# Eight shared PSUM banks, global scores on 544 columns, and another order for the last batch of a fused attention and mixture kernel

## Chip, cores and metric

The kernel runs on one core of a Trainium2 chip. The metric is device time in microseconds (us) for one execution; lower is better. Engines are named as in the profile: PE (matmul; PEld is its weight load), DVE, ACT, POOL, and SP, which issues DMAs. The profile comes from one execution; the times come from others.

## What is computed

Two stages for 8 batches, all in f32. The first is attention with 8 heads of 64 dimensions: 512 local positions see 32 global positions and a band of 32 to each side; 32 global positions see everything. The second takes the 544 x 512 result through four experts of causal attention with 64 dimensions each, of which the two with the highest gate values count.

```python
# stage 1, per batch and head (scale = 1/8)
s_g  = scale * q_g @ concat(k_g, k_l).T            # 32 x 544, no mask
out_g = softmax(s_g) @ concat(v_g, v_l)
s_l  = concat(scale * q_l @ k_g.T, where(|i-j| <= 32, scale * q_l @ k_l.T, -1e9))
out_l = softmax(s_l) @ concat(v_g, v_l)
x = concat(out_g, out_l)                           # 544 x 512 over the heads
# stage 2, per batch
gates = top-2 softmax of x @ w_gate
for e in range(4):
    a = softmax(causal(scale * (x @ wq[e]) @ (x @ wk[e]).T))
    out += gate[e] * (a @ (x @ wv[e]) @ wo[e])
```

## The kernel before

**Order.** The kernel first records every operation with `op` (engines allowed, planned ns, a function, the buffers it reads and writes, a priority), and then `Plan.place` issues them one by one. PE's operations are issued in exactly the order in which they were written. For DVE, ACT, POOL and SP the planner picks, by its planned times, the operation that could start first, ties going to the lower priority. Each engine then runs its queue in that order on the chip, waiting by semaphores. Planned times set the order alone.

**Buffers.** A `Ring` has so many slots, and a `Buf` takes a slot when its first operation is placed and gives it back after its last. PSUM has eight banks of 512 f32 per partition. Before the change they are two rings: `sc`, two buffers of two banks each, for the scores of stage 1 (`sp`) and 2 (`msp`); and `w`, four buffers of one bank for all else:

```python
    sc_ring, w_ring = Ring(2, loose=True), Ring(4, loose=True)
    def scores(name):
        return Buf(sc_ring, lambda: psum.tile([128, 2, 512], F32, tag="sc", name=name, bufs=2))
    def ps(shape, name):
        return Buf(w_ring, lambda: psum.tile(shape, F32, tag="w", name=name, bufs=4))
```

**Steps.** `step(s)` writes stage 1 for pair s of heads (32 pairs, four to a batch) and, six steps later, stage 2 of a batch in four steps r = 0 to 3, with the rest of the batch before (`old`) still to be done: scores of its second two experts (c = 1) in r = 0 and 1, products in r = 1 and 3, outputs in r = 3. Within a step, `whole` weaves short transposes (`turns`) among long projections (`products`).

**Stage 1 of a pair.** `kn` and `qn` become `kd` and `qp` (DVE's 32x32 transposes; in the first four pairs PE's `px`). `kd` holds groups of 96 local keys and the 32 global keys again (POOL copies `kg` there), 128 columns a group, so that 96-wide windows and the global keys are one operand. PE: `sp` (L515). DVE takes the band and the row minimum of each 128 columns (L527), ACT the exponential (L530). A step later PE transposes (`pt`, L545), ACT or DVE copies to `ptw` (L238 for ACT, L240 for DVE; all copies have these lines), and a step after that PE forms `xq` (L564), DVE scales it to `xn` (L568), PE turns it (`xp`, L579), and ACT and DVE split it into high and low parts `xh` (L249) and `xl` (L250). The values `v` are spread by POOL copies (L240).

**Global queries.** Every second step, `p1_global_scores` multiplies two pairs' global queries (`qb`) with the 640 columns of `kd` (`spg`, L625): 512 columns in one bank, in which the global keys come again in groups 1 to 3 and are masked out by `gmask` (DVE, L628), and 128 in another (L632). ACT's exponential covers 640 columns (L637). `long_turn` transposes five chunks of 128 (`pga`, L653), copied to `longt`; `p1_global_av` (L674) multiplies with `v`.

**Stage 2 of a batch.** `pqk` (L704) gives `kt`, `qt`; `pv` (L741, L752) the values; `m_gates` a chain of small DVE operations on `xt` (L777 to L806), with the ranking at L784 to L791. The score tiles t = 0, 1, 2 of a pair of experts hold the query blocks (0 and 1), (2), (3), so 128 and 256, 384 or 512 columns: PE `msp` (L833), DVE `pm` with the causal mask (L847), ACT's exponential (L851), DVE's sums and reciprocals `msm` (L854, L856), POOL's scaling with the gate (L862), PE's `mpt` (L886), copies to `mptw`, PE's `yp` (L905), ACT's `yh` and DVE's `yl`. The last 32 positions of all four experts, the tail, take their own way: `tsp` (L926, DVE L929 and L933), one exponential (L941), `long_turn`, `yt` (L965), `turned` (L591), `tt` (L597), `yth`, `ytl`. `out_tile` multiplies with `wo` (`po`, L984), ACT copies (`ot`) and issues the output DMA (L991): four tiles a batch, and a tail tile for four batches with four DMAs.

**The end.** After the last batch's r = 3 there is nothing left to lie beside it. It writes in this order: tail product, all of `yp` for c = 1, the tail's turn, four output tiles, the tail's output tile.

Of the kernel before, what the change touches and what calls it, by code (L numbers as in the profile page):

```python
# [1 line left out]

# [192 lines left out]
def fused_kernel(ctx: ExitStack, tc: tile.TileContext, q_l, k_l, v_l, q_g, k_g, v_g,  # L195
# [144 lines left out]

    def setup_gmask():
        def f(e):
            nc.gpsimd.memset(gmask, 0.0)
            nc.gpsimd.memset(gmask[:, 1:, 96:], NEG)
        op("POOL", 800, f, w=["gmask"])
# [155 lines left out]
    def p1_scores(k):  # L501
# [6 lines left out]
        def f(e):  # L508
            for t in range(4):
                for g in range(4):  # L510
                    u = 4 * t + g
                    c = col(window(u))
                    for h in range(2):
                        rows = slice(64 * h, 64 * h + 64)
                        nc.tensor.matmul(sp.t[32 * g:32 * g + 32, h, 128 * t:128 * t + 128],  # L515
                                         qp.t[rows, 32 * u:32 * u + 32], kd.t[rows, c:c + 128],
                                         start=True, stop=True)
# [91 lines left out]
    def p1_global_scores(b, g):  # L609


        qb = G[b]["qb"]
        sg = buf("long", [128, 5, 128])
        sm = buf("sgm", [128, 8], 3)
        kdl = [PR[b * NP + 2 * g + j]["kd"] for j in range(2)]
        for half in range(2):
            sp = ps([128, 4 - 3 * half, 128], "spg")

            def f(e, half=half, sp=sp):
                for j in range(2):  # L620
                    p, kd, out_ = 2 * g + j, kdl[j].t, sp.t[64 * j:64 * j + 64].rearrange("p c s -> p (c s)")
                    parts = [(out_, kd[:, :512])] if half == 0 else [(out_[:, :96], kd[:, 512:608]),
                                                                     (out_[:, 96:], kd[:, 640:])]
                    for o_, k_ in parts:
                        nc.tensor.matmul(o_, qb.t[:, p, :], k_, start=True, stop=True)  # L625
            op("PE", 950 - 700 * half, f, r=[qb, *kdl], w=[sp])
            if half == 0:
                op("DVE", 610, lambda e, sp=sp: nc.vector.tensor_tensor_reduce(  # L628
                    out=sg.t[:, :4], in0=sp.t, in1=gmask, scale=-SCALE, scalar=BIG,
                    op0=ALU.add, op1=ALU.min, accum_out=sm.t[:, 0:1]), r=[sp, "gmask"], w=[(sg, 0), (sm, 0)])  # L630
            else:
                op("DVE", 210, lambda e, sp=sp: nc.vector.tensor_scalar(  # L632
                    sg.t[:, 4], sp.t[:, 0], -SCALE, None, op0=ALU.mult, op1=ALU.min, accum_out=sm.t[:, 1:2]), r=[sp],
                   w=[(sg, 1), (sm, 1)])
        op("DVE", 100, lambda e: nc.vector.tensor_reduce(sm.t[:, 2:3], sm.t[:, 0:2], axis=AX.X, op=ALU.min),
           r=[(sm, 0), (sm, 1)], w=[(sm, 2)], late=20)
        op("ACT", 825, lambda e: nc.scalar.activation(sg.t, sg.t, AF.Exp, bias=sm.t[:, 2:3], scale=-1.0,  # L637
                                                      accum_out=sm.t[:, 3:4]), r=[sg, (sm, 2)], w=[sg, (sm, 3)], late=30)
# [517 lines left out]
```

## Time and profile before

| | |
|---|---|
| median of 3 runs (lowest, highest) | 554.78 us (554.69, 556.05) |
| profiled execution: own time, span | 553.77 us, 552.0 us |
| mean clock granted to PE | 0.994 of full |
| DMA: packets, MB | 190792, 41.83 |
| PE's idle time, summed over the windows 0:50, 50:500, 500:530, 530:552 | 14.6, 16.1, 0.6, 8.0 us |

Instructions carry the line of `kernel.py` and the program's names, `out<-in`. A timeline row is: start, length, engine, line, operation, names, shape, count, and in brackets how long the engine had been idle and what ended that. A waits row is: who waited, for whom, us in total, times, longest. PE's ends are modelled, so matmuls overlap in the rows. In the trace an f32 matmul is two instructions of PE (a transpose is one).

### The profile page before, as it was taken

The numbers are of one execution on the slowest core, as the hardware profiler recorded it, in microseconds if no ns is written. First come the engines' busy times: TensorE is split into PE (matmuls) and PEld (weight loads), VectorE is DVE, ScalarE is ACT, GpSimd is POOL, SyncE is SP. The second block draws the span as 40 slices with busy tenths as digits, with TensorE's granted clock in tenths as the row PEclk, the third lists the DMA queues.
The fourth block names the chain that finished last, engine by engine and source line by source line (L and its number), as shares of the span: only waits on it lengthen the run. The fifth ranks groups of instructions, "written<-read, shape, count | busy, mean of one in ns | idle before, by whom it ended". The sixth has DMA issues, their size and how long they took to land.

```text
span 552.0 us, 22219 instructions
## 1 busy us (share of the span) xinstructions
PE 512.7 (93%) x8796; PEld 425.4 (77%) x8796; DVE 413.8 (75%) x1713; ACT 323.2 (59%) x1146; POOL 287.7 (52%) x526
## 2 busy tenths in 40 slices
PE   4887999899999999998999999999999999999976
PEld 3666976778878887887878787788878888788754
DVE  6999879778777887779786896778877775565550
ACT  1767548866466745755675763667457464542552
POOL 6988579874193745648175642927437212231230
PEclk9989999999999999999999999999999999999989
DMA  9786585462262513533163422624122000200202
GB/s 178 144 148 129 111 160 101 86 114 42 53 149 55 95 22 70 146 70 50 25 136 87 84 34 57 145 54 78 22 48 80 2 2 2 78 2 1 77 2 95
DMA packets 190792, 41.83 MB, mean 76 GB/s; under 512 B 186080, under 2 KB 186080, under 8 KB 190688
## 3 DMA queue, kind: packets, MB, share of 16 engines
q1 hardware_dynamic: 174448, 29.12, 28.8%
q10 hardware_dynamic: 16240, 11.29, 6.7%
q8 instruction: 69, 1.13, 0.9%
q14 instruction: 35, 0.29, 0.2%
HBM read 31.47 MB, written 8.91 MB: 73 GB/s over the span
## 4 chain that ended last, share of the span: by engine, by line
PE 65%; DVE 11%; ACT 9%; DMA 5%; POOL 4%; issue 3%; SPq 2%; POOLq 0%; DVEq 0%; ACTq 0%
PE pqk L704 13%; PE pv L741 8%; PE po L984 7%; PE msp L833 6%; PE xq L564 5%; PE mpt L886 5%; PE yp L905 4%; PE sp L515 4%; POOL v L240 3%; PE pt L545 3%; PE spg L625 2%; ACT st L530 2%; DMA v<-in_v_l_dram 2%; PE xp L579 2%; PE pga L653 2%
## 5 line engine op out<-in xcount | busy, mean ns | idle before, releaser
L240 POOL COPY v<-v 32x512 f32<-32x512 f32 (+2 forms) x192 | 116.3, 606 | 46.6 <-DMA v<-in_v_l_dram 36.1
L862 POOL TENSOR_SCALAR pm<-pm,msm,gate 128x512 f32<-128x512 f32 (+3 forms) x128 | 76.9, 614 | 119.8 <-DVE msm L856 86.3
L530 ACT ACTIVATE st<-st,sm 128x128 f32<-128x128 f32 x256 | 100.4, 395 | 35.2 <-DVE sm L527 26.9
L240 POOL COPY v<-vg 32x640 f32<-32x640 f32 (+1 forms) x96 | 65.9, 686 | 38.5 <-PE xg L674 26.8
L851 ACT ACTIVATE pm<-pm,msm 128x512 f32<-128x512 f32 (+3 forms) x128 | 70.6, 554 | 22.9 <-DVE msm L847 22.8
L847 DVE CUSTOM_DVE_ANT_0 pm<-msp,cmask 128x512 f32<-128x512 f32 (+3 forms) x128 | 56.9, 486 | 11.2 <-PE msp L833 11.2
L527 DVE CUSTOM_DVE_ANT_0 st<-sp,band 128x128 f32<-128x128 f32 x256 | 58.1, 285 | 9.4 <-PE sp L515 9.4
L886 PE MATMUL mpt<-ident,pm 128*128 128x128 f32 x320 | 48.1, 276 | 7.1 <-DVE kt L240 3.4
L886 PEld LDWEIGHTS mpt<-ident,pm 128*128 128x128 f32 x320 | 36.5, 141 | 16.2 <-POOL pm L862 5.5
L530 ACT ACTIVATION_READ_ACCUMULATOR st<-st,sm 128x1 f32 x256 | 48.7, 190 | 0.0
L833 PE MATMUL msp<-kt,qt 64*64 64x384 f32 (+3 forms) x512 | 46.1, 448 | 0.5 <-DVE qt L240 0.5
L515 PE MATMUL sp<-kd,qp 64*32 64x128 f32 x2048 | 39.6, 283 | 3.9 <-issue 1.8
L564 PEld LDWEIGHTS xq<-v,ptw 128*32 128x32 f32 x2048 | 30.7, 111 | 14.8 <-issue 6.2
L564 PE MATMUL xq<-v,ptw 128*32 128x64 f32 x2048 | 36.2, 223 | 5.6 <-ACT ptw L238 2.7
L905 PE MATMUL yp<-mptw,vt 128*64 128x128 f32 x640 | 40.1, 278 | 0.3 <-issue 0.3
L704 PE MATMUL pqk<-xh,wk_hi 128*128 128x272 f32 x128 | 39.6, 309 | 0.3 <-DVE xl L604 0.3
L545 PE MATMUL pt<-ident,st 128*128 128x128 f32 x256 | 36.4, 274 | 3.5 <-DVE xl L250 3.2
L704 PE MATMUL pqk<-xh,wq_hi 128*128 128x272 f32 x128 | 39.7, 310 | 0.0
L238 ACT COPY mptw<-mpt 128x512 f32<-128x512 f32 (+1 forms) x51 | 23.9, 487 | 26.2 <-PE mpt L886 25.6
L741 PE MATMUL pv<-wv_hi,xh 128*128 128x260 f32 x128 | 38.6, 301 | 0.7 <-DVE xl L250 0.7
L905 PEld LDWEIGHTS yp<-mptw,vt 128*64 128x64 f32 x640 | 36.2, 139 | 1.7 <-issue 0.7
L704 PE MATMUL pqk<-xl,wq_hi 128*128 128x272 f32 x128 | 36.9, 288 | 0.0
(166 smaller groups left out, 1365.9 us busy)
## 6 DMA issues: line engine op xcount, KB each, us to landing
out_dram<-ot ACTq DMA_DIRECT2D x32, 256.0 KB, 2.1
v<-in_v_l_dram SPq DMA_DIRECT2D x62, 120.0 KB, 3.2
kn<-in_k_l_dram SPq DMA_DIRECT2D x109, 64.0 KB, 2.7
qn<-in_q_l_dram SPq DMA_DIRECT2D x109, 64.0 KB, 2.4
v<-in_v_l_dram SPq DMA_DIRECT2D x59, 32.0 KB, 2.5
vg<-in_v_g_dram SPq DMA_DIRECT2D x21, 64.0 KB, 2.2
qn<-in_q_l_dram ACTq DMA_DIRECT2D x5, 128.0 KB, 2.7
ot<-in_q_g_dram SPq DMA_DIRECT2D x8, 64.0 KB, 2.2
```

The costliest lines, as they stand in the source:

```text
L240: ENG[e].tensor_copy(out, in_)
L515: nc.tensor.matmul(sp.t[32 * g:32 * g + 32, h, 128 * t:128 * t + 128], qp.t[rows, 32 * u:32 * u + 32], kd.t[rows, c:c + 128], start=True, ...
L527: op("DVE", 211, lambda e, h=h, t=t, i=i: nc.vector.tensor_tensor_reduce(out=st.t[:, h, t], in0=sp.t[:, h, 128 * t:128 * t + 128], in1=ban ...
L530: op("ACT", 385, lambda e, h=h, t=t, i=i: nc.scalar.activation(st.t[:, h, t], st.t[:, h, t], AF.Exp, bias=sm.t[:, 0, i:i + 1], scale=-1.0, ...
L564: nc.tensor.matmul(xq.t[32 * g:32 * g + 32, t, h, :], pts[h].t[:, 32 * u:32 * u + 32], v.t[:, h, window(u), :], start=True, stop=True)
L704: nc.tensor.matmul(pp.t, w[:, ch, cols], x(part, ch)[:, n], start=(ch == 0 and w is hi and part == 0), stop=(ch == NCH - 1 and part == 1))
L741: nc.tensor.matmul(pv.t, x(part, ch)[:, 128 * i:128 * i + 128], w[:, ch, :], start=(ch == 0 and part == 0 and w is hi), stop=(ch == NCH - ...
L833: nc.tensor.matmul(sp.t[64 * u:64 * u + 64, x, at:at + n], qt.t[rows, q0:q0 + 64], kt.t[rows, :n], start=True, stop=True)
L851: op("ACT", 280 + 0.83 * n, lambda e, x=x, at=at, n=n, s=s: nc.scalar.activation(pm.t[:, x, at:at + n], pm.t[:, x, at:at + n], AF.Exp, bia ...
L862: op("POOL", 240 + 0.83 * n, lambda e, x=x, at=at, n=n, i=i, s=s: nc.gpsimd.tensor_scalar(pm.t[:, x, at:at + n], pm.t[:, x, at:at + n], sm ...
L886: nc.tensor.transpose(pt.t[:, k, :], pm.t[:, x, at + 128 * j:at + 128 * j + 128], ident)
L905: nc.tensor.matmul(yp.t[64 * x:64 * x + 64, 128 * i:128 * i + 128], vt.t[:, j, 64 * (2 * c + x):64 * (2 * c + x) + 64], flat[:, where[x, i ...
```

## The change

There are three parts.

1. One ring of eight banks, made once as fixed tiles. `ps` gives any bank a view of the wanted shape, and `scores` is a list of two such buffers, one for each head (or expert) of the pair. The ring picks the free slot whose planned end is longest ago.
2. The global scores are taken on 544 columns: 416 in the first bank (128 of group 0, then 96 of each of groups 1 to 3, read from `kd` with gaps), 128 in the second. There is no `gmask`; DVE's first operation becomes a `tensor_scalar` with a minimum, as the second was. The exponential covers 544 columns. The transposes are of 128, 96, 96, 96 and 128 columns (`CHUNKS`), and the copy to `longt` is split, since the 96-row chunks fill only 96 partitions; the products over these chunks run over 96 partitions.
3. For the last batch alone: the 384-wide tile of c = 1 is written in r = 0 and not in r = 1; the scaling of its c = 1 probabilities may go to DVE or POOL; `yp` for c = 1 is in two halves with the tail's turn between them; the tail's output tile comes first.

```diff
-                    b.tile = ring.fixed[b.slot] if ring.fixed else b.make()
+                    if ring.fixed:
+                        b.tile = ring.fixed[b.slot]
+                        if b.make:
+                            b.tile = b.make(b.tile)
+                    else:
+                        b.tile = b.make()
...
-    sc_ring, w_ring = Ring(2, loose=True), Ring(4, loose=True)
+    banks = [psum.tile([128, 512], F32, name=f"bank{i}", bufs=1) for i in range(8)]
+    ring = Ring(8, loose=True, fixed=banks)
+    def ps(shape, name):
+        def view(bank):
+            t = bank[:, :math.prod(shape[1:])]
...
+        return Buf(ring, view)
     def scores(name):
-        return Buf(sc_ring, lambda: psum.tile([128, 2, 512], F32, tag="sc", name=name, bufs=2))
+        return [ps([128, 512], name) for _ in range(2)]
...
-        for half in range(2):
-            sp = ps([128, 4 - 3 * half, 128], "spg")
+        for half, n in ((0, 416), (1, 128)):
+            sp = ps([128, n], "spg")
...
+                    if half == 0:
+                        parts = [(o_[:, :128], kd[:, :128]),
+                                 (o_[:, 128:].rearrange("p (c s) -> p c s", s=96),
+                                  kd[:, 128:512].rearrange("p (c s) -> p c s", s=128)[:, :, :96])]
+                    else:
+                        parts = [(o_[:, :96], kd[:, 512:608]), (o_[:, 96:], kd[:, 640:])]
...
+    CHUNKS = ((0, 128), (128, 96), (224, 96), (320, 96), (416, 128))
...
+        rows = min(rows for _, rows in some)
+        evac(lambda: pt.t[:rows, 4 * part:4 * part + n, :], lambda: pa.t[:rows], 128 * n, [pa], [(pt, part)])
+        if rows < 128:
+            evac(lambda: pt.t[rows:, 0, :], lambda: pa.t[rows:, 0, :], 128, [pa], [(pt, "g")])
...
+                engs = "POOL|DVE" if b == B - 1 and c == 1 else "POOL"
...
+        for some in ((0, 1), (2, 3)) if between else (range(4),):
...
+            if between and n0 == 0:
+                between()
...
+        end = r == 3 and old == B - 1
...
-            m_av(old, 1)
+            m_av(old, 1, M[old, "turn"] if end else None)
...
-        if has(first[0]):
+        if has(first[0]) and not (r == 1 and old == B - 1):
...
-                products += [lambda: m_out_tail(old // 4)]
+                products.insert(0 if end else 4, lambda: m_out_tail(old // 4))
...
+        if r == 0 and old == B - 1:
+            m_scores(old, 1, 1)
+            m_softmax(old, 1, 1)
```

**What moves in the queues.** PE's order changes only in the last batch. Its last stretch up to the first output tile was:

```order
L833 MATMUL msp<-kt,qt 64x256 x4
L905 MATMUL yp<-mptw,vt 64x128 x20
L926 MATMUL tsp<-kt,qtbd_78 64x512 x2
L926 MATMUL tsp<-kt,qtbd_78 64x32 x2
L833 MATMUL msp<-kt,qt 64x384 x4
L886 MATMUL mpt<-ident,pm 128x128 x20
L653 MATMUL pga<-ident,long 128x128 x5
L965 MATMUL yt<-vt,longt 32x64 x20
L905 MATMUL yp<-mptw,vt 64x128 x20
L597 MATMUL tt<-ident,turned 128x128
L984 MATMUL po<-wo_hi,yh 128x512
```

and from behind `tsp` on it is now (each PSUM buffer carries its bank's name, 64 to 71; L903 is `mpt`, L666 `pga`, L987 `yt`, L927 `yp`, L604 `tt`, L1006 `po`):

```order
L903 MATMUL bank_66<-ident,pm 128x128 x4
L903 MATMUL bank_71<-ident,pm 128x128 x4
L903 MATMUL bank_68<-ident,pm 128x128 x4
L903 MATMUL bank_64<-ident,pm 128x128 x2
L903 MATMUL bank_67<-ident,pm 128x128 x4
L903 MATMUL bank_65<-ident,pm 128x128 x2
L666 MATMUL bank_66<-ident,long 128x128 x4
L666 MATMUL bank_71<-ident,long 128x128
L987 MATMUL bank_69<-vt,longt 32x64 x20
L927 MATMUL bank_70<-mptw,vt 64x128 x6
L604 MATMUL bank_68<-ident,turned 128x128
L927 MATMUL bank_64<-mptw,vt 64x128 x14
```

The 384-wide `msp` has gone from here to a place ahead of `yp`, the tail's `tt` stands between the halves of the last `yp`, and each unit of work takes another bank, the one longest unused.

DVE's queue over the same stretch, from the reads of the last score tile on, before:

```order
L854 TENSOR_SCALAR msm<-msm 128x2
L856 RECIPROCAL msm<-msm 128x2
L854 TENSOR_SCALAR msm<-msm 128x4
L856 RECIPROCAL msm<-msm 128x4
L250 TENSOR_TENSOR yl<-yp,yh 128x512
L929 TENSOR_SCALAR long,tsm<-tsp 128x512
L933 ISA long,tsm<-tsp,tmask 128x32
L933 ISA tsm 128x1
L847 ISA pm,msm<-msp,cmask 128x384
```

and now (L861 is the read of `msp`, L868 and L870 are `msm`, L879 the scaling with the gate, L951 the read of `tsp`, L265 `yl`):

```order
L861 ISA pm,msm<-bank_67,cmask 128x384
L861 ISA msm 128x1
L868 TENSOR_SCALAR msm<-msm 128x2
L870 RECIPROCAL msm<-msm 128x2
L879 TENSOR_SCALAR pm<-pm,msm,gate 128x512
L868 TENSOR_SCALAR msm<-msm 128x4
L870 RECIPROCAL msm<-msm 128x4
L951 TENSOR_SCALAR long,tsm<-bank_65 128x512
L879 TENSOR_SCALAR pm<-pm,msm,gate 128x256
L868 TENSOR_SCALAR msm<-msm 128x2
L265 TENSOR_TENSOR yl<-bank_69,yh 128x512
```

The read of the 384-wide tile has come ahead of the 512-wide tile's `msm`, and one half of each scaling is DVE's.

In every batch the planner also orders DVE, ACT and POOL a little differently. The place that the prediction speaks of is DVE's queue in the gates of a batch (step r = 1), before:

```order
L785 TENSOR_TENSOR xt<-vt 128x80
L936 TENSOR_REDUCE tsm<-tsm 128x1
L495 STREAM_TRANSPOSE kd_71<-kn 128x5x96
L496 STREAM_TRANSPOSE kd_71<-kn 128x32
L240 COPY kt<-pqk 128x272
L789 TENSOR_TENSOR xt<-xt,before 128x80
L790 TENSOR_TENSOR xt<-xt 128x80
L791 TENSOR_REDUCE xt<-xt 128x20
L533 TENSOR_SCALAR sm<-sm 128x8
```

and now (L803 is the second half of the ranking, L502 the transpose to `kd`):

```order
L799 TENSOR_TENSOR xt<-vt 128x80
L958 TENSOR_REDUCE tsm<-tsm 128x1
L255 COPY mptw<-bank_71 128x512
L803 TENSOR_TENSOR xt<-xt,before 128x80
L804 TENSOR_TENSOR xt<-xt 128x80
L805 TENSOR_REDUCE xt<-xt 128x20
L540 TENSOR_SCALAR sm<-sm 128x8
L502 STREAM_TRANSPOSE kd_79<-kn 128x5x96
L503 STREAM_TRANSPOSE kd_79<-kn 128x32
L255 COPY mptw<-bank_64 128x512
```

Two copies of `mptw` have come from ACT, the transposes to `kd` stand behind the ranking, and the copies of `kt` have gone to ACT.

More of the change, by code (lines that the diff above doesn't have):

```diff
@@ L339, in setup_masks @@
         op("POOL", 2800, f, w=["masks"])
[L341 to L345, printed above, removed]
     VW = E * D + E
@@ L612, in p1_global_scores @@
         qb = G[b]["qb"]
-        sg = buf("long", [128, 5, 128])
+        sg = buf("long", [128, 640])
         sm = buf("sgm", [128, 8], 3)
         kdl = [PR[b * NP + 2 * g + j]["kd"] for j in range(2)]
-        for half in range(2):
-            sp = ps([128, 4 - 3 * half, 128], "spg")
+        for half, n in ((0, 416), (1, 128)):
+            sp = ps([128, n], "spg")
             def f(e, half=half, sp=sp):
                 for j in range(2):
[L621 to L634, printed above, removed]
@@ new lines, in f @@
+                    p, kd, o_ = 2 * g + j, kdl[j].t, sp.t[64 * j:64 * j + 64]
+                    if half == 0:
[4 more added lines that the diff above has]
+                        parts = [(o_[:, :96], kd[:, 512:608]), (o_[:, 96:], kd[:, 640:])]
+                    for to, k_ in parts:
+                        nc.tensor.matmul(to, qb.t[:, p, :], k_, start=True, stop=True)
@@ L644, in p1_global_scores, with long_turn @@
         G[b, g] = dict(sg=sg, sm=sm)
-    def long_turn(src, key, where, part):
-        n = 4 - 3 * part
+    CHUNKS = ((0, 128), (128, 96), (224, 96), (320, 96), (416, 128))
+    def long_turn(src, key, where, part, chunks):
+        some = chunks[4:] if part else chunks[:4]
+        n = len(some)
         pa = ps([128, n, 128], "pga")
-        def f(e):
-            for j in range(n):
-                nc.tensor.transpose(pa.t[:, j, :], src.t[:, 4 * part + j], ident)
-        op("PE", 30 + 110 * n, f, r=[src], w=[pa])
         if part == 0:
@@ L892, in m_ptrans_units, with m_av @@
         return units
-    def m_av(b, c):
+    def m_av(b, c, between=None):
         vt = M[b, "v"]
         pts = {i: (M[b, c, t, "pt"], M[b, c, t, "where"]) for t in range(3) for i, _ in TILES[t]}
-        yp = ps([128, SL], "yp")
-        def f(e):
-            for i in range(4):
-                pt, where = pts[i]
-                flat = pt.t.rearrange("p a j q -> p (a j) q")
-                for j in range(i + 1):
-                    for x in range(2):
-                        nc.tensor.matmul(yp.t[64 * x:64 * x + 64, 128 * i:128 * i + 128],
-                                         vt.t[:, j, 64 * (2 * c + x):64 * (2 * c + x) + 64],
-                                         flat[:, where[x, i, j], :], start=(j == 0), stop=(j == i))
-        op("PE", 2350, f, r=[vt, *{id(p): p for p, _ in pts.values()}.values()], w=[yp])
         if c == 0:
@@ L911, in m_av, with f @@
         y = M[b, "yo"]
-        high_low(lambda part: y[part].t[:, c, :], lambda: yp.t, 512, [yp], (y[0], c), (y[1], c))
+        for some in ((0, 1), (2, 3)) if between else (range(4),):
+            n0, n = 128 * some[0], 128 * len(some)
+            yp = ps([128, n], "yp")
+            def f(e, some=some, yp=yp, n0=n0):
+                for i in some:
+                    pt, where = pts[i]
+                    flat = pt.t.rearrange("p a j q -> p (a j) q")
+                    for j in range(i + 1):
+                        for x in range(2):
+                            nc.tensor.matmul(yp.t[64 * x:64 * x + 64, 128 * i - n0:128 * i - n0 + 128],
+                                             vt.t[:, j, 64 * (2 * c + x):64 * (2 * c + x) + 64],
+                                             flat[:, where[x, i, j], :], start=(j == 0), stop=(j == i))
+            op("PE", 235 * sum(i + 1 for i in some), f, r=[vt, *{id(pts[i][0]): pts[i][0] for i in some}.values()], w=[yp])
+            high_low(lambda part, n0=n0, n=n: y[part].t[:, c, n0:n0 + n], lambda yp=yp: yp.t, n, [yp],
+                     (y[0], (c, n0)), (y[1], (c, n0)))
+            if between and n0 == 0:
+                between()
     def m_tail_scores(b):
@@ L954, in m_tail_turn @@
     def m_tail_turn(b, part):
-        long_turn(M[b, "ptail"], (b, "pttail"), M, part)
+        long_turn(M[b, "ptail"], (b, "pttail"), M, part, [(128 * j, 128) for j in range(5)])
     def m_tail_av(b):
@@ L994, in m_out @@
     def m_out(b, i):
-        y = M[b, "yo"]
-        out_tile(y, lambda part, c: y[part].t[:, c, 128 * i:128 * i + 128],
+        y = [(t, (c, n0)) for t in M[b, "yo"] for c in range(2) for n0 in ((0, 256) if b == B - 1 and c == 1 else (0,))
+             if n0 == 0 or i > 1]
+        out_tile(y, lambda part, c: M[b, "yo"][part].t[:, c, 128 * i:128 * i + 128],
                  [(out[b, 128 * i:128 * i + 128, :], slice(0, 128))])
@@ L1054, in step @@
             turns.append(G[bb, p // 2]["turn"])
+        end = r == 3 and old == B - 1
         if r == 3 and has(old):
             m_tail_av(old)
-            turns.append(M[old, "turn"])
+            if not end:
+                turns.append(M[old, "turn"])
         if at(s) and s % 2 == 1:
```

59 lines of the change are left out of this document (36 added, 23 removed).

## The prediction

> **What bounds the kernel now.** I read the page's first part, then the table of windows, then the waits of TensorE.
>
> ```profile
> PE 512.7 (93%) x8796; PEld 425.4 (77%) x8796; DVE 413.8 (75%) x1713; ACT 323.2 (59%) x1146; POOL 287.7 (52%) x526
> 0.00:50.00 50.00, 35.42 (x864) 27.54 (x864) 42.47 (x194) 25.84 (x107) 41.57 (x86) 0.97 0.81 154
> 200.00:250.00 50.00, 48.69 (x882) 40.25 (x881) 38.45 (x158) 31.25 (x112) 24.57 (x45) 1.00 0.40 86
> 530.00:540.00 10.00, 6.72 (x95) 5.70 (x96) 3.24 (x12) 2.93 (x10) 1.31 (x2) 0.83 0.01 2
> 540.00:552.00 12.00, 7.31 (x31) 5.18 (x29) 1.04 (x3) 3.67 (x8) 0.00 (x0) 1.00 0.31 109
> ```
>
> In the windows, the columns after the length are PE, PEld, DVE, ACT and POOL busy, then clock, DMA share and GB/s. There are three stages. In the first 50 us the DMA engines are 81% busy and PE idles 14.6 us. Between 50 and 530 PE is almost never idle, so the sum of PE's work and PE's short stops sets the time. From 530 on PE idles 3.3 and 4.7 us, part of it at a lowered clock. What the short stops are:
>
> ```profile
> PE mpt L886 <- DVE kt L240: 3.4, 4, 1.2
> PE pt L545 <- DVE xl L250: 3.2, 5, 0.6
> PE po L984 <- ACT ot L238: 2.4, 4, 0.6
> ...
> 185.25 0.60 PE L545 MATMUL pt<-ident,st 128*128 128x128 f32 x4
> 185.74 0.69 DVE L250 TENSOR_TENSOR xl<-xp,xh 128x512 fp32r<-128x512 f32 x1
> 186.49 0.66 PE L545 MATMUL pt<-ident,st 128*128 128x128 f32 x4 [0.63 <-DVE xl L250]
> ```
>
> `pt` transposes `st`; it needs neither `xl` nor, in `mpt`, `kt`. What these matmuls wait for is the PSUM buffer: DVE's `xl` is the last reader of `xp`, `kt` that of an old `pqk`, `ot` that of an old `po`. All three come from the ring of four buffers (`w`), while the two buffers of two banks each for scores (`sc`) stand apart. These rows hold 9.0 us in 13 stops. A stop costs more than its idle time, because ends are modelled: the four matmuls in 0.60 us, each 0.27 us long, start 0.11 us apart, so the next was due at 185.69 and came at 186.49, which is 0.80 and not 0.63. With 0.17 us more for each, the 13 stops cost **11.2 us**. That is the ceiling of the first part.
>
> **The change, part by part.** *Banks.* The four-buffer ring becomes eight single banks that scores and all else share; a score tile is two of them, each given back by itself. In the written order of step r=1, `pt`'s second half stands on the bank that the first half of `sp` left. In DVE's order the reads of `sp` are over before `xl` starts at 185.74, and `xp` is read until `xl` ends at 186.43. The wait thus goes, and what is late next is DVE:
>
> ```profile
> 185.00:195.00 10.00, 8.96 (x73) 8.53 (x72) 9.57 (x35) 7.60 (x27) 9.12 (x17) 1.00 0.41 66
> 225.00:230.00 5.00, 5.00 (x147) 3.36 (x147) 2.73 (x16) 2.08 (x8) 4.57 (x9) 1.00 0.53 146
> ...
> 195.24 1.10 PE L564 MATMUL xq<-v,ptw 128*32 128x64 f32 x64
> 195.76 0.43 DVE L240 COPY qt<-pqk 128x272 f32<-128x272 f32 x1
> 196.41 0.69 DVE L568 TENSOR_TENSOR xn<-xq,sm 128x512 f32<-128x512 f32 x1 [0.21 <-PE xq L564]
> 198.38 0.66 PE L579 MATMUL xp<-ident,xn 128*128 128x128 f32 x4
> ```
>
> From 185 to 195 DVE works 9.57 of 10 us, and its queue is free only at 196.19. A PE that comes earlier still gets `xn` no sooner than 196.2+0.7, so `xp` can move forward by 1.5 us at most, of the 0.8 (`pt`) plus about 0.9 (`mpt`) that stop PE there. At the end of step r=3 (225 to 230) DVE has room, and the 0.8 of `po` come through whole. That would be some 9.5 us. DVE's, ACT's and POOL's queues are reordered a little at many places, and some new stop must be expected, so I take three quarters of the ceiling, **8.5 us**; the ends are 0 and 14 (the ceiling plus short stops that no row above names).
>
> *Global scores.* A group of `spg` takes PE from its first start to that of the next line:
>
> ```profile
> 210.97 1.38 PE L625 MATMUL spg<-kd,qgbd 128*64 128x512 f32 x12
> 212.13 2.43 PE L905 MATMUL yp<-mptw,vt 128*64 128x128 f32 x40
> 214.49 0.80 PE L515 MATMUL sp<-kd,qp 64*32 64x128 f32 x38
> ```
>
> 1.16 us go to 640 columns for each of two pairs. With 544 columns that is 0.99, so 0.17 is saved. Two matmuls more (four in the trace, where each f32 matmul is two) cost at most four times the 0.06 of a `yp` matmul (2.36 us for 40), halved since the pairs run side by side: 0.12. The saving is 0.05 to 0.17; I take 0.14, nearer to the row of this very line. Of 16 groups the first two lie in the start, so 14 count: **2.0 us** (0.7 to 2.4). The operands of the new 288-column matmul have gaps in SBUF, which no matmul of the trace has; a rival below prices that.
>
> ```profile
> L628 DVE CUSTOM_DVE_ANT_0 long<-spg,gmask 128x512 f32<-128x512 f32 x16 | 10.9, 682 | 1.7 <-PE spg L625 1.1
> L632 DVE TENSOR_SCALAR_CACHE_REDUCE long<-spg 128x128 f32<-128x128 f32 x16 | 4.4, 275 | 0.0
> L637 ACT ACTIVATE long<-long,sgm 128x640 f32<-128x640 f32 x16 | 13.2, 827 | 25.8 <-DVE sgm L635 25.8
> L941 ACT ACTIVATE long<-long,tsm 128x544 f32<-128x544 f32 x8 | 5.9, 740 | 1.7 <-DVE tsm L936 1.7
> L238 ACT COPY longt<-pga 128x128 f32<-128x128 f32 x18 | 4.8, 267 | 16.1 <-PE pga L653 15.9
> ```
>
> The reduction of 416 columns lies between 682 and 275 ns, 0.58 by the line through both: DVE saves 1.6 us in all. The exponential takes 740 instead of 827: ACT saves 1.4. Added are 16 copies of 32 rows, each as the 267 ns row: 4.3 us, mostly on ACT, which is 59% busy. All of it lies beside PE and counts as nothing; if ACT were the late engine, 4.3-1.4 = 2.9 us would show. `gmask` leaves POOL's first microseconds, where DVE's masks and then DMA are late: nothing.
>
> *The end.* PE is stopped where the last probabilities come from POOL:
>
> ```profile
> 525.50 0.16 DVE L854 TENSOR_SCALAR msm<-msm 128x2 f32<-128x2 f32 x1
> 526.06 1.52 POOL L862 TENSOR_SCALAR pm<-pm,msm,gate 128x512 f32<-128x512 f32 x2 [6.96 <-DVE msm L856]
> 528.02 1.96 POOL L862 TENSOR_SCALAR pm<-pm,msm,gate 128x128 f32<-128x128 f32 x4 [0.43 <-DVE msm L856]
> 529.51 0.55 DVE L847 CUSTOM_DVE_ANT_0 pm<-msp,cmask 128x384 f32<-128x384 f32 x1
> 532.86 1.19 PE L886 MATMUL mpt<-ident,pm 128*128 128x128 f32 x6 [2.39 <-POOL pm L862]
> 535.36 1.29 PE L965 MATMUL yt<-vt,longt 128*32 128x64 f32 x40 [0.77 <-DVE longt L240]
> 539.81 0.48 PE L984 MATMUL po<-wo_hi,yh 128*128 128x512 f32 x1
> 27.63 0.69 DVE L368 CAST wv_hi<-mptw 128x1040 fp32r<-128x1040 f32 x1
> 535.00:536.00 1.00, 0.64 (x25) 0.67 (x29) 0.22 (x1) 0.00 (x0) 0.00 (x0) 0.50 0.00 0
> ```
>
> The 384-wide tile's scores now stand ahead of `yp` and `tsp`, so DVE reads them by 526.5 instead of 530.1 (its second read now starts at 529.51); the 512 tile's `msm` follows a microsecond later than now, at 526.5, but DVE scales one half of each tile. Such a 512 scaling from SBUF to SBUF has no row; the nearest, 0.69 for 1040 columns and 0.69 for `xn`'s 512, put it between 0.35 and 0.7, and I take 0.5. Following the queues as they stand: POOL's 512 ends at 527.8, its 128s at 528.9, its 256 at 529.5, its 384 at 530.8 (DVE's at 530.5); PE's last six `mpt` start at 530.9; the long exponential, behind ACT's copies, runs 531.0 to 531.9; `longt` is ready at 533.1 and `yt` starts at 533.3, **2.1 us** earlier. Then the clock: in the half-clock window `yt`, `yp` and `tt` take 535.36 to 539.81, where `po` begins, 4.45 us; at full clock `yt`'s 40 matmuls take about 0.6 (as at 535.36 with half the time), `yp` 2.36 (above), `tt` 0.1, together 3.0. PE no longer stands 2.4 us in one piece, so I take the full clock: **1.5 us**.
>
> [...]
>
> ```profile
> 547.35 0.59 ACT L238 COPY ot<-po 128x512 f32<-128x512 f32 x1 [0.81 <-PE po L984]
> 547.96 1.76 ACTq L991 DMA_DIRECT2D out_dram<-ot  x4
> out_dram<-ot ACTq DMA_DIRECT2D x32, 256.0 KB, 2.1
> out_dram<-ot ACTq DMA_DIRECT2D x8, 64.0 KB, 2.0
> ```
>
> The tail's output moves from last to first. Its operands `ytl` are ready while `yp`'s second half runs, its four DMA issues (1.76 us on ACT's queue) lie beside the next `po`, and the last thing is one issue: three issues of 0.44 us leave the end, **1.3 us**, and the larger transfer takes back 0.1. Together the end gives 2.1+1.5+1.2 = **4.8 us** (2.5 to 6.5).
>
> Sum: 8.5+2.0+4.8 = 15.3 from the profiled execution's 553.77 gives 538.5. The median of the runs shown, 554.78, is 1.0 above that execution, so **539.5 us**.
>
> **Rivals.** (1) *DVE's bursts keep what the banks free.* For it speaks the 9.57 of 10 us above; against it that DVE idles elsewhere (2.73 of 5). Then only 2.0+4.8 remain, and perhaps 1 of the banks: 547. (2) *The banks give more than the named stops*, since PE may now run ahead everywhere: 14+2.4+6 gives 532. (3) *The gapped operand slows the matmul.* If 288 columns ran at half speed, a group would cost 1.16x288/640 = 0.52 more, 14 times: 7.3 us, so 546. [...] (4) *Slower: DVE waits for PE in its burst.* In the changed order DVE has a copy of `mptw` (0.69 us) between the first and the second half of the gates' ranking, where `kt` and `kd` stood; it waits for PE's `mpt`, and behind it stand the rest of the gates, `kd`, `msm` and `xn`. PE now does that `mpt` just as DVE gets there:
>
> ```profile
> 188.49 0.60 PE L886 MATMUL mpt<-ident,pm 128*128 128x128 f32 x4
> 189.16 0.14 DVE L936 TENSOR_REDUCE tsm<-tsm 128x1 f32<-128x2 f32 x1
> ```
>
> If `mpt` came over 1.4 us later than DVE there, 6.5 batches would lose 9 us and more, against the 6.8 of the other parts and 1.7 for the bound: some 558. Against it: PE comes earlier there, not later. (5) *The banks rotate but the planner's order waits as before, and the end's clock falls:* 2.0+1.2 less some new stops, within 0.3%.
>
> **How the numbers follow.** The forecast has 0.50, (1) 0.20, (2) 0.12, (3) 0.05, (4) 0.08, (5) 0.05. 0.3% of the median is 1.7 us, about what a measurement of this kernel can tell from no change. Faster are the forecast, (1), (2) and (3): 0.87; within it (5): 0.05; slower (4): 0.08. The unknowns' ends give 553.77-14-2.4-6.5+1.0 = 532 and 553.77-0-0.7-2.5+1.0 = 551.6; the range 531 to 549 leaves out (4), (5) and a little beyond both ends.
>
> **What would show it.** Right: the waits `pt<-xl`, `po<-ot` and `mpt<-kt` are gone from PE's list and a batch's period is some 1.3 us shorter (8.5 over 6.5 batches); a group of `spg` takes about 1.0 us; `yt` follows the last six `mpt` by 2.4 us at a granted clock of 1.0; the span ends with a single output DMA. Wrong: new waits of PE on `xn`, `kd` or `msm` in the burst (rival 1), a `spg` group of over 1.3 us (rival 3), DVE idle before `mptw` (rival 4), a granted clock of 0.5 near the end.

## The result and the profile after

The changed kernel takes **530.84 us** (median of 4 runs, 529.93 to 532.62), the kernel before 554.74 in the same comparison: a ratio of 0.956, 95% interval 0.9534 to 0.9587. That is 23.9 us less, where 15.3 were forecast, and 0.2 us below the low end of the forecast's range. In the middle stage PE now works 375.8 of 379 us; it worked 367.3 before. First the busy line of the page after, then one window, 121 to 500 us, of the kernel before and of the changed one (columns as in the prediction):

```profile
PE 500.6 (95%) x8860; PEld 428.3 (81%) x8860; DVE 404.3 (76%) x1715; ACT 325.3 (62%) x1165; POOL 284.4 (54%) x521
```

```profile
121.00:500.00 379.00, 367.29 (x6153) 308.89 (x6152) 291.96 (x1188) 226.61 (x792) 182.17 (x334) 1.00 0.29 62
```

```profile
121.00:500.00 379.00, 375.77 (x6394) 326.07 (x6393) 290.90 (x1221) 238.08 (x840) 186.23 (x342) 1.00 0.29 63
```

PE's waits in the changed kernel (who waited for whom, us, times, longest; every PSUM buffer is called `bank` now, L571 is `xq`, L401 `pg`, L847 `msp`, L492 `px`, L522 `sp`, L586 `xp`):

```profile
PE bank L571 <- ACT ptw L253: 4.3, 2, 2.6
PE bank L401 <- DMA ot<-in_k_g_dram: 3.5, 1, 3.5
PE bank L847 <- DVE qt L255: 2.2, 4, 0.7
PE bank L492 <- DMA kn<-in_k_l_dram: 2.1, 1, 2.1
PE bank L522 <- issue: 2.1, 3, 1.6
PE bank L586 <- DVE xn L575: 1.9, 2, 1.6
```

The three that the prediction named are gone. What is left in the middle is mainly the wait of `msp` (L847) for `qt`: four times, 2.2 us, where the kernel before had it once, 0.53 us in its last batch. PE's timeline at the place that the prediction went through (step r=1, there 185 to 198 us; `pt` is L552, `pqk` L718, `mpt` L903):

```profile
182.42 1.04 PE L552 MATMUL bank<-ident,st 128*128 128x128 f32 x8
183.21 0.37 PE L718 MATMUL bank<-xh,wk_hi 128*128 128x272 f32 x1
...
186.75 1.03 PE L903 MATMUL bank<-ident,pm 128*128 128x128 f32 x8
...
191.98 1.16 PE L522 MATMUL bank<-kd,qp 64*32 64x128 f32 x64
193.64 1.09 PE L847 MATMUL bank<-kt,qt 64*64 64x512 f32 x8 [0.51 <-DVE qt L255]
```

The eight `pt` are one row, and the next group starts 0.79 us after their start, where it was 1.64.

PE's order is the same in both kernels up to the last batch, so every group of matmuls can be set beside itself: the time from its first start to that of the next group, before less after. A positive number is time gained. Summed over the groups that start between 121 and 500 us in the kernel before, in us:

| groups | changed kernel | only the banks (next section) |
|---|---|---|
| `pt`: ten of 0.85 to 0.89 (waits on `xl` and, behind `po`, on `ot`), one 0.19 | 8.9 | 8.9 |
| `pqk` with the `mpt` behind it: 1.33, 1.27, 0.86, 0.70, 0.56 | 4.75 | 4.8 |
| `pga`, `mpt`, `tt`: twenty of 0.12 to 0.37 and smaller ones | 4.25 | 4.1 |
| `spg`: ten of 0.15 to 0.16 | 1.55 | 0 |
| `sp` ahead of a late `qt`: -0.80, -0.58, -0.42, and +0.30 | -1.5 | -1.45 |
| all others | 0.6 | 0.1 |
| **sum** | **18.6** | **16.4** |

The two spans differ by 23.1 us: these 18.6, less 0.6 which the first 121 us take more, and 5.1 of the end. A group of `spg` (L635; L927 is `yp`) and the end of the changed kernel, with `yt` at L987, `po` at L1006:

```profile
207.74 1.23 PE L635 MATMUL bank<-kd,qgbd 128*64 128x128 f32 x16
208.75 1.50 PE L927 MATMUL bank<-mptw,vt 128*64 128x128 f32 x23
```

```profile
512.22 1.08 PE L903 MATMUL bank<-ident,pm 128*128 128x128 f32 x6 [0.40 <-DVE tsm L958]
514.53 0.77 PE L987 MATMUL bank<-vt,longt 128*32 128x64 f32 x40 [0.57 <-ACT longt L253]
517.97 0.50 PE L1006 MATMUL bank<-wo_hi,yth 128*128 128x512 f32 x1
525.27 0.58 ACT L253 COPY ot<-bank 128x512 f32<-128x512 f32 x1 [0.80 <-PE bank L1006]
525.89 0.34 ACTq L1013 DMA_DIRECT2D out_dram<-ot  x1
```

```profile
513.00:516.00 3.00, 2.43 (x60) 1.83 (x58) 1.63 (x6) 1.10 (x4) 0.00 (x0) 1.00 0.00 0
```

The group takes 1.01 us. `yt` follows the last six `mpt` by 2.3 us, at a granted clock of 1.00, and one output DMA ends the program.

### The profile page after: what moved, and what is told of

Same layout as the page of the kernel before. It is cut to its first block, busy times and chain, and to the rows that moved or that the text cites. A ratio compares the mean times of both kernels' runs of the same rounds, so it can differ in the third digit from the quotient of the medians.

```text
span 528.9 us, 22393 instructions
## 1 busy us (share of the span) xinstructions
PE 500.6 (95%) x8860; PEld 428.3 (81%) x8860; DVE 404.3 (76%) x1715; ACT 325.3 (62%) x1165; POOL 284.4 (54%) x521
## 4 chain that ended last, share of the span: by engine, by line
PE 75%; DVE 13%; DMA 4%; SPq 3%; ACT 2%; issue 2%; POOL 0%; ACTq 0%; DVEq 0%; POOLq 0%
PE bank L718 14%; PE bank L1006 9%; PE bank L755 8%; PE bank L847 7%; PE bank L927 6%; PE bank L903 6%; PE bank L571 5%; PE bank L522 4%; PE bank L552 3%; PE bank L635 3%; SPq L271 3%; PE bank L586 2%; PE bank L666 2%; DMA v<-in_v_l_dram 2%; DVE st L534 2%
## 5 line engine op out<-in xcount | busy, mean ns | idle before, releaser
L879 POOL TENSOR_SCALAR pm<-pm,msm,gate 128x512 f32<-128x512 f32 (+3 forms) x125 | 74.9, 611 | 114.5 <-DVE msm L870 87.5
L861 DVE CUSTOM_DVE_ANT_0 pm<-bank,cmask 128x512 f32<-128x512 f32 (+3 forms) x128 | 56.7, 485 | 11.0 <-PE bank L847 10.4
L534 DVE CUSTOM_DVE_ANT_0 st<-bank,band 128x128 f32<-128x128 f32 x256 | 57.8, 284 | 6.1 <-PE bank L522 6.1
L903 PE MATMUL bank<-ident,pm 128*128 128x128 f32 x320 | 46.7, 274 | 1.5 <-DVE msm L870 0.6
L847 PE MATMUL bank<-kt,qt 64*64 64x384 f32 (+3 forms) x512 | 45.6, 448 | 2.2 <-DVE qt L255 2.2
L571 PEld LDWEIGHTS bank<-v,ptw 128*32 128x32 f32 x2048 | 30.9, 111 | 16.7 <-issue 8.1
L571 PE MATMUL bank<-v,ptw 128*32 128x64 f32 x2048 | 36.8, 223 | 7.0 <-ACT ptw L253 4.3
L522 PE MATMUL bank<-kd,qp 64*32 64x128 f32 x2048 | 39.5, 283 | 3.9 <-issue 2.1
L903 PEld LDWEIGHTS bank<-ident,pm 128*128 128x128 f32 x320 | 36.9, 140 | 7.8 <-POOL pm L879 2.7
L718 PE MATMUL bank<-xh,wk_hi 128*128 128x272 f32 x128 | 39.6, 310 | 0.0
L718 PE MATMUL bank<-xh,wq_hi 128*128 128x272 f32 x128 | 39.5, 308 | 0.0
L927 PE MATMUL bank<-mptw,vt 128*64 128x128 f32 x640 | 39.1, 275 | 0.0
L755 PE MATMUL bank<-wv_hi,xh 128*128 128x260 f32 x128 | 38.5, 301 | 0.0
L718 PE MATMUL bank<-xh,wq_lo 128*128 128x272 f32 x128 | 36.9, 289 | 0.0
L718 PE MATMUL bank<-xl,wk_hi 128*128 128x272 f32 x128 | 36.9, 288 | 0.0
L718 PE MATMUL bank<-xl,wq_hi 128*128 128x272 f32 x128 | 36.9, 288 | 0.0
L718 PE MATMUL bank<-xh,wk_lo 128*128 128x272 f32 x128 | 36.9, 288 | 0.0
```

Of the source, the lines that this page charges most:

```text
L522: nc.tensor.matmul(sp[h].t[32 * g:32 * g + 32, 128 * t:128 * t + 128], qp.t[rows, 32 * u:32 * u + 32], kd.t[rows, c:c + 128], start=True, ...
L571: nc.tensor.matmul(xq.t[32 * g:32 * g + 32, t, h, :], pts[h].t[:, 32 * u:32 * u + 32], v.t[:, h, window(u), :], start=True, stop=True)
L718: nc.tensor.matmul(pp.t, w[:, ch, cols], x(part, ch)[:, n], start=(ch == 0 and w is hi and part == 0), stop=(ch == NCH - 1 and part == 1))
L755: nc.tensor.matmul(pv.t, x(part, ch)[:, 128 * i:128 * i + 128], w[:, ch, :], start=(ch == 0 and part == 0 and w is hi), stop=(ch == NCH - ...
L847: nc.tensor.matmul(sp[x].t[64 * u:64 * u + 64, at:at + n], qt.t[rows, q0:q0 + 64], kt.t[rows, :n], start=True, stop=True)
L879: lambda e, x=x, at=at, n=n, i=i, s=s: ENG[e].tensor_scalar(pm.t[:, x, at:at + n], pm.t[:, x, at:at + n], sm.t[:, 3, s:s + 1], gate.t[:, i ...
```

## Experiments

Times are medians with the ratio to the kernel before and its 95% interval; each comparison timed the kernel before anew (medians 554.7 to 555.5 us). The two last columns are from each run's profile: the first to the last `pv` matmul, and from there to the end of the span. The first of them depends on how far DMA had come at the first `pv` (49 to 56 us), so a difference of a microsecond between two kernels in it means little. The last one is of a single execution too; the four runs six, joint, qt_act and q_act, whose end is written as the changed kernel's, lie within 0.1 us of its 60.5.

| kernel | time, us | ratio | `pv` to `pv` | to the end |
|---|---|---|---|---|
| before | 554.74 | 1 | 435.7 | 65.5 |
| changed | 530.84 | 0.956 (0.9534 to 0.9587) | 418.1 | 60.5 |
| banks_only | 539.77 | 0.9738 (0.9699 to 0.9777) | 418.1 | 66.5 |
| spg_only | 551.34 | 0.9918 (0.9885 to 0.9951) | 431.4 | 66.1 |
| end_only | 551.75 | 0.9931 (0.9903 to 0.996) | 434.1 | 62.3 |
| four_four | 548.5 | 0.9877 (0.9841 to 0.9914) | 430.8 | 63.2 |
| order44 | 531.98 | 0.9579 (0.954 to 0.9617) | 418.9 | 61.1 |
| six | 536.59 | 0.9656 (0.9609 to 0.9703) | 423.5 | 60.5 |
| joint | 531.87 | 0.9578 (0.9543 to 0.9614) | 419.2 | 60.5 |
| qt_act | 532.72 | 0.9585 (0.9543 to 0.9626) | 419.0 | 60.5 |
| q_act | 529.55 | 0.9554 (0.9525 to 0.9584) | 417.0 | 60.4 |
| end_pool, end_noearly, end_oldorder | 529.58, 533.84, 532.77, one run each | | 417.1, 418.5, 418.9 | 61.6, 64.0, 61.4 |

### Each part alone

*banks_only* is the kernel before with part 1 of the change, *spg_only* with part 2, *end_only* with part 3.

```diff
# banks_only
-    sc_ring, w_ring = Ring(2, loose=True), Ring(4, loose=True)
+    ring = Ring(8, loose=True, fixed=banks)
# spg_only
-        for half in range(2):
-            sp = ps([128, 4 - 3 * half, 128], "spg")
+        for half, n in ((0, 416), (1, 128)):
+            sp = ps([128, n], "spg")
# end_only
+        end = r == 3 and old == B - 1
...
+            m_av(old, 1, M[old, "turn"] if end else None)
```

> Only the first part of the change: one ring of eight single banks; global scores on 640 columns with the mask, old order of the end. Theory A, the prediction's term (three quarters of the named stops, 8.5 us): about 546.2, ratio 0.985. Theory B, the comparison of the two traces (every named stop goes whole, 13.4 us in 15 stops, and small ones of 0.14 to 0.23 with them, less 1.8 of new stops; 14 us): about 540.7, ratio 0.975. Under B the waits of pt, of mpt on kt and of po on ot are all gone from TensorE's list.

> Only the second part: 544 columns for the global scores, old PSUM rings, old end. Prediction's term: 2.0 us less, about 552.7, ratio 0.996, and a group of spg 1.0 us instead of 1.16. Rival: with four buffers the split copy of the transposed chunks (ACT or DVE) holds the PSUM buffer longer and takes part of it back, 553.5 to 555; or, if the 3.5 us that the two traces differ by at spg are all of its own, about 551.2.

> Only the third part: the last batch's order, old PSUM rings, 640 columns. Prediction's term 4.8 us: about 549.9, ratio 0.991. Rival: the early 384-wide tile and the split yp need buffers which the old rings don't have, so that half of it or more is lost: 551 to 553.

The banks alone take 15.7 us off the 555.46 of the kernel before in this comparison (interval of the ratio: 12 to 17 us), and 16.4 in the groups' table: theory B, all stops go whole. The three gains, 15.7, 4.1 and 3.7, add up to 23.5, about the whole change's; the sum hides that the second is larger alone and the third smaller than in the whole change.

*spg_only* saves what the group says, 0.16 for each, but the rival is there too. DVE's, ACT's and PE's rows in that run (L885 is `mpt`, L240 a DVE copy, L238 an ACT copy):

```profile
137.80 0.68 DVE L240 COPY longt<-pga 96x512 f32<-96x512 f32 x1
138.51 0.26 ACT L238 COPY longt<-pga 32x128 f32<-32x128 f32 x1 [0.43 <-DVE longt L240]
139.63 0.27 ACT L238 COPY longt<-pga 128x128 f32<-128x128 f32 x1
139.95 0.44 PE L885 MATMUL mpt<-ident,pm 128*128 128x128 f32 x2 [0.31 <-ACT longt L238]
```

ACT's copy of the last 32 rows starts only when DVE's copy of the first 96 is over. With four buffers the copies of `pga` thus hold a buffer so long that `mpt` waits, five times, each 0.45 us more than before. The whole of it is still 4.1 us (2.7 to 6.4 by the interval) and not 2, since other stops moved. Over the groups from 121 to 500 us the trace gains 3.1: 1.55 at `spg`, 2.1 at `pt` and 1.5 at `pqk`, less 2.1 at `mpt`. Why `pt` and `pqk` moved wasn't followed further.

*end_only* gains 3.2 us from the last `pv` to the end, not 4.8, and its time of 551.75 us is the rival's: with the old rings PE stops 0.81 us among the last `mpt` and 1.03 ahead of `pga`, in the changed kernel 0.40 and not at all. The old end on eight banks (banks_only) takes 66.5, so with them the same edits come to 6.0. About 0.9 of that is the clock of the one execution profiled: it stood at 0.50 for 6.8 us there and for 3.4 in the kernel before, and the last `mpt`, `pga` and `yp` took 0.14, 0.36 and 0.44 us longer.

### Is it sharing, the number of banks, or the order?

*four_four* keeps eight single banks, each given back by itself, but in two rings. *order44* has the changed kernel's buffers with four_four's queues on DVE, ACT, POOL and SP: the planner first runs through without issuing, with two rings of four, and its order is then issued with the ring of eight. *six* takes two banks away. *joint* lets the two banks of a score tile become free together.

```diff
# four_four
-    ring = Ring(8, loose=True, fixed=banks)
+    ring = Ring(4, loose=True, fixed=banks[:4])
+    sc_ring = Ring(4, loose=True, fixed=banks[4:])
...
-        return [ps([128, 512], name) for _ in range(2)]
+        return [ps([128, 512], name, sc_ring) for _ in range(2)]
# order44
-        plan.place(globals().get("PLAN_LOG"))
+        plan.place(globals().get("PLAN_LOG"), plan.order_with(
+            {"w": Ring(4, loose=True, fixed=[None] * 4), "sc": Ring(4, loose=True, fixed=[None] * 4)}))
# six
-    ring = Ring(8, loose=True, fixed=banks)
+    ring = Ring(6, loose=True, fixed=banks[:6])
# joint (and the same with sp[x] in the second stage)
-    ... r=[sp[h], ("band", t)] ...
+    ... r=[*sp, ("band", t)] ...
```

> The changed kernel, but the eight single banks are two rings of four: one for the scores, one for all else; each half of a score tile is still given back by itself and the planner still picks the slot that is free longest. Theory A, sharing is what counts: the stops of pt, mpt and po return, 13 to 14 us, so 543 to 545. Theory B, single release and the choice of the slot are what counts: within 2 us of the changed kernel, 531 to 533.

> The changed kernel's eight shared banks, but with the order of work on DVE, ACT, POOL and SP that the planner makes for two rings of four (that of the run four_four, instruction for instruction). Theory A, the stops were waits for a buffer at run time: they go, 531 to 534. Theory B, the planner's better order for DVE and ACT has half of the gain: 536 to 545.

> The changed kernel with six banks in the shared ring instead of eight. Theory A, what counts is that work which is not scores can use the scores' banks while they are free: most of the stops stay away, 532 to 538. Theory B, the number of banks counts: a score tile in flight holds two, so four are left as before, and the stops return, 542 to 548.

> The changed kernel, but for the planner the two banks of a score tile become free together, when the last read of both is over. If giving back each bank by itself counts: 534 to 540. If eight banks are enough without it: 530 to 532.

In four_four the stops are back, in the same places, and 548.5 us is above even theory A's 543 to 545; five waits of `mpt` for the split copy, each 0.45 us longer than in the kernel before, as in spg_only, cost 2.3 us of that. PE's timeline there, where `pt` (L553) again stands behind `xl`:

```profile
184.86 0.60 PE L553 MATMUL bank<-ident,st 128*128 128x128 f32 x4
185.99 0.66 PE L553 MATMUL bank<-ident,st 128*128 128x128 f32 x4 [0.53 <-DVE xl L266]
```

In order44, with the same queues on the other engines, they are gone (L582 is `pt`, L748 `pqk`):

```profile
181.10 1.03 PE L582 MATMUL bank<-ident,st 128*128 128x128 f32 x8
181.89 0.37 PE L748 MATMUL bank<-xh,wk_hi 128*128 128x272 f32 x1
```

So the stops were waits for a buffer while the program ran. The planner's other order of DVE and ACT had next to no part in it (531.98 against 530.84, intervals overlapping), and giving back each bank by itself in the planner's account had none that shows (531.87; the edit touches that account alone, not what an instruction reads). By groups, of the 18.6 us that the changed kernel gains from 121 to 500 us, order44 keeps 17.2, joint 18.1, six 13.5 and four_four 3.0, of which 1.55 are the groups of `spg`. Six shared banks keep most of the gain, two rings of four little of it: what counts is that short work may use a bank that scores have left. With six it is mainly one new kind of stop that costs, in the group of `tt` (L604): four groups 0.70 to 0.79 us longer than in the kernel before, where the next matmul, `po`, waits for DVE's `turned`, which it doesn't read:

```profile
216.82 0.27 PE L604 MATMUL bank<-ident,turned 128*128 128x128 f32 x1
217.56 0.50 PE L1006 MATMUL bank<-wo_hi,yh 128*128 128x512 f32 x1 [0.46 <-DVE turned L598]
```

### The wait that came in: qt

Around the wait for `qt` in the changed kernel, DVE's and ACT's queues:

```profile
192.50 0.61 DVE L820 COPY gt<-gate 32x1 f32<-32x1 f32 x4
193.15 0.44 DVE L255 COPY qt<-bank 128x272 f32<-128x272 f32 x1
193.50 0.68 DVE L575 TENSOR_TENSOR xn<-bank,sm 128x512 f32<-128x512 f32 x1
```

```profile
193.62 0.37 ACT L253 COPY qtbd<-bank 64x32 f32<-64x32 f32 x2 [3.62 <-DVE qt L255]
```

DVE comes to the copy only behind the gates, and ACT stands idle for 3.62 us in front of two other copies out of the same bank. ACT had this wait in the kernel before too (waits row below), where PE waited for `qt` only once:

```profile
ACT qtbd L238 <- DVE qt L240: 22.7, 9, 3.8
```

Two runs move the copies. *qt_act* gives the copy of 272 columns to ACT, *q_act* all three:

```diff
# qt_act
-        evac(lambda: t.t[:, n], lambda: pp.t, HS, [pp], [(t, half)])
+        evac(lambda: t.t[:, n], lambda: pp.t, HS, [pp], [(t, half)], "ACT" if kind == "q" and half == 1 else "ACT|DVE")
# q_act: the same, and for the two copies of 32 columns too
+        engs = "ACT" if kind == "q" and half == 1 else "ACT|DVE"
...
+                     lambda rows=rows: pp.t[rows, HS - SG:], 32, [pp], [(qt, (c, x_))], engs)
```

> The changed kernel with the copy of qt's second half (272 columns) always on ACT instead of ACT or DVE. TensorE waits four times, 2.2 us in all, for that copy, which stands behind the gates in DVE's queue while ACT idles 3.6 us. If those waits go and nothing else is late: 528.6, ratio to the kernel before some 0.4 points lower than the changed kernel's 0.956. Rival: xn on DVE, then right behind, is the next bound, and 0 to 0.5 us are left: 530 to 531.

> The changed kernel with all three copies out of the bank of qt's second half (272 columns and twice 32) on ACT. In the run qt_act one of them stayed on DVE, and ACT's copy waited for it (3.87 us idle before the copy). Theory A, a copy waits for another engine's earlier copy out of the same bank: with all three on ACT the waits of TensorE for qt go from the list, 2 to 3 us, so 528 to 529. Theory B, qt is late for another reason or xn behind it is the next bound: 530 to 531.

qt_act gained nothing: PE waited 3.0 us for `qt`, now on ACT. In its queues, DVE's row first, ACT's copy of `qt` waits for DVE's copy of 32 columns, which had stayed behind the gates:

```profile
257.26 0.18 DVE L255 COPY qtbd<-bank 64x32 f32<-64x32 f32 x1
257.47 0.39 ACT L253 COPY qt<-bank 128x272 f32<-128x272 f32 x1 [3.87 <-DVE qtbd L255]
```

The traces show 3.62 and 3.87 us of idle ACT, each ended by the other engine's read of that bank and of the same partitions, 0.03 us ahead of ACT's copy. With all three on ACT, q_act's copy runs at 191.09 and `msp` starts without a wait, 1.09 us behind `sp`:

```profile
192.01 1.16 PE L522 MATMUL bank<-kd,qp 64*32 64x128 f32 x64
193.10 1.09 PE L848 MATMUL bank<-kt,qt 64*64 64x512 f32 x8
```

Three of PE's four waits for `qt` are gone; one of 0.47 us is left, in the last batch. Group by group the three give back 0.57, 0.80 and 0.42 us. The time, 529.55 at a ratio of 0.9554, can't be told from the changed kernel's 0.956. So the theory holds for the wait; that it is worth 2 us is not shown.

### The end, step by step

```diff
# end_pool
-                engs = "POOL|DVE" if b == B - 1 and c == 1 else "POOL"
+                engs = "POOL"
# end_noearly
-        if has(first[0]) and not (r == 1 and old == B - 1):
+        if has(first[0]):
...
-        if r == 0 and old == B - 1:
-            m_scores(old, 1, 1)
-            m_softmax(old, 1, 1)
# end_oldorder
-            if not end:
-                turns.append(M[old, "turn"])
+            turns.append(M[old, "turn"])
...
-            m_av(old, 1, M[old, "turn"] if end else None)
+            m_av(old, 1)
...
-                products.insert(0 if end else 4, lambda: m_out_tail(old // 4))
+                products.insert(4, lambda: m_out_tail(old // 4))
```

> The changed kernel, but POOL alone scales the last batch's last probabilities. From the first pv of the last batch's group to the end of the span the changed kernel takes 60.8 us. By the prediction's steps POOL's queue (1.5 us for the 512, twice 0.5 for the 128s, 0.6 and 0.8 for halves) then sets the last mpt again: about 2 us more, 62.8. Rival: the stop lowers the clock as well, 64 to 65.

> The changed kernel, but the last batch's 384-wide tile at its old place behind tsp. By the prediction DVE's two reads of it (0.55 us each) then come behind tsp's reads and the 384's scaling follows 1 to 2 us later: 62 to 63 us for the stretch that takes 60.8. Rival: with eight banks the place of a score tile does not matter, 60.8 to 61.3.

> The changed kernel, but yp of the last batch in one piece behind the tail's turn as before, and the tail's output tile last. By the prediction three DMA issues (1.3 us, less 0.1) come back at the end, and the tail's turn stands ahead of yp as in the kernel before: 62.0 us for the stretch that takes 60.8. Rival: the turned tail is waited for as well, some 0.5 us more: 62.5.

The stretch in the table starts at the last `pv` matmul, 0.3 us behind the expectations' start: 60.5 us in the changed kernel. Without DVE's share of the scaling (one each of the 512-, 384- and 256-wide pieces; the 128-wide ones are all POOL's) it is 1.1 longer (about 2 expected), with the late 384-wide tile 3.5 (1.2 to 2.2 expected), with the old order 0.9 (1.2 expected). The late tile costs twice over. Its row, then a window behind it, from end_noearly:

```profile
514.44 1.52 PE L903 MATMUL bank<-ident,pm 128*128 128x128 f32 x6 [3.02 <-POOL pm L879]
```

```profile
514.50:517.50 3.00, 2.53 (x11) 2.13 (x11) 1.66 (x3) 0.64 (x2) 0.00 (x0) 0.50 0.00 0
```

PE stands still for 3.0 us, and then works three microseconds at half the clock.

## Why the forecast was too small

**What bounds the kernel: right.** PE's short stops for PSUM buffers set the middle's time; as they go, PE is busy 99% of it (375.8 of 379).

**Banks: the mechanism right, the size wrong, and this is the step that failed.** The prediction took 8.5 us, with 14 as the upper end; from 121 us on the banks alone gave 16.4. Four pieces of the difference of 7.9:

- *"I take three quarters of the ceiling"*: nothing was kept back of the named stops. 2.7 us.
- *The ceiling of 11.2*: the named waits cost 13.7 in 16 places. A stop at `pt` came to 0.85 to 0.89 and not 0.80, which makes 0.6 us over the 13 named, and three more places, 1.8 us, weren't in the rows that were summed. 2.5 us in all.
- *Stops that no row named*: `pga`, `mpt` and `tt` had 0.12 to 0.37 us each time, 4.1 us in all and 0.3 in other groups. Most are too short to stand in a list of waits; a group's length beside its best length elsewhere shows it. The prediction had these only in its upper end, with 2.8.
- *"Some new stop must be expected"*: right, 1.7 us (1.45 ahead of `qt`, 0.25 at `yt`).

8.5 + 2.7 + 2.5 + 4.4 - 1.7 is the 16.4. *What is late next is DVE* was right as a place: in the one step r=1 that was worked through, 0.85 and 0.56 went at `pt` and `mpt` (0.8 and about 0.9 were put there), and 0.58 came back. But it was `qt` behind the gates, ahead of `msp`, and not `xn` that was late.

**Global scores: right.** 0.15 to 0.16 us a group against 0.14, over 14 groups 2.2 us against 2.0. The copies of 32 rows that were counted as nothing cost nothing on eight shared banks; with four buffers they cost five waits of 0.45 us (spg_only).

**The end: right in the sum, 5.1 against 4.8, though less neatly in its parts.** `yt` follows `mpt` by 2.3 us (2.4 forecast), the clock stays at 1.00, the old order is worth 0.9 (1.2 forecast). Counted from the same `msp` group (500.89 us before, 482.85 in the changed kernel), `yt` starts 2.8 us earlier (2.1 forecast), the way from `yt` to `po` is 1.0 shorter (1.5 forecast as the clock's part), and that from `po` to the end 1.3 (1.2). By the runs that take out one edit each, the early tile is the largest piece: 3.5 us with its clock, and DVE's share of the scaling 1.1. These overlap and are not to be added. The term also hung on the first part, which the prediction didn't foresee: 3.2 us with the old rings, about 5 with eight banks. That the clock stays full once PE no longer stands 2.4 us in one piece, on which the 1.5 us rest, was the author's estimate, and no run shows it as a rule: in the changed kernel the clock stayed at 1.00 up to the last matmul, with stops of at most 0.57 us in this stretch, but in four_four it fell to 0.50 behind three of 0.43, 0.34 and 0.77 us (last section).

**Rivals.** (2), that the banks give more, is what happened: 532 was its time, 530.84 was measured, and it had 0.12; even its 14 us for the banks were less than the 16.4. (1), (5): the waits went, and the clock stayed at 1.00. (3): half speed was the author's assumption, and no run shows it; a group with the gapped operand takes 1.01 us where half speed would have given 1.5 (and a time of 547, not 546, with the 1.0 us that the other sums add). (4): DVE's copy of `mptw` starts at 186.34, right behind its neighbour, and DVE did not wait for PE there.

## What to carry to other kernels

A waits list shows a shortage of buffers by its releaser: where PE waited for the last reader of something that it did not need, it was a buffer here. When the buffer came, the whole stop went, 0.85 to 0.89 us each at `pt`. Sum such stops by the length of each group beside its shortest repetition, since the stops too short for the list were a quarter of the gain here. Before adding buffers, share those there are: six banks in one ring did better (0.966) than eight in two (0.988).
